# Six of batch 0's last groups are moved from ahead of the tile loop into tiles 0 to 3, and batch 1's first input loads are issued between filter copies

## The chip, the cores and the metric

One Trainium2 chip, one core. The metric is the device time of one execution in microseconds (us), lower is better. Names of engines in the profile: PE is TensorE's matmuls and PEld its weight loads, DVE is VectorE, ACT is ScalarE, POOL is GpSimd and SP is SyncE, which issues most of the DMAs.

## The reference

A global filter over the sequence in the frequency domain, then a two-layer network with exact GELU over every token:

```
x: (8, 3008, 256); filt_r, filt_i: (1505, 256); w_in: (256, 2048); w_out: (2048, 256); all float32
X = rfft(x, axis=1)
Y = X * (filt_r + 1j * filt_i)
y = irfft(Y, n=3008, axis=1)
h = y.reshape(24064, 256) @ w_in
g = 0.5 * h * (1 + erf(h / sqrt(2)))
out = g @ w_out            # (24064, 256) float32
```

## The kernel before

**The filter as matmuls.** 3008 = 47 × 64, so a transform of one batch goes in four matrix stages. For batch 0 they are called c1, c2, c3 and c4, and stand ahead of the network with nothing of the network beside them; the order of the instructions is written out by hand. c1 turns input columns by a table, c1t transposes on PE, c2 multiplies by the second table, and DVE's product with the filter (L569) follows it. c3 turns back and leaves its result in the tile vt. Then come eight groups u = 0 to 7. For each, c3t(u) makes eight 128 × 128 transposes on PE, which DVE copies to a tile d (L605). c4(u) makes two halves of four matmuls of 94 columns on d, and each half is written to a ring of mixed tokens (376 columns a group, channels on the partitions) by ACT or DVE (L620). The filter tile F is loaded by POOL's DMAs to half of the partitions, and dup_filters copies it to the other half, two planes a copy, mostly on POOL.

**Later batches.** Batches 1 to 7 use s1, s2, s3 and s4, in slots amid the network. fold adds and subtracts input halves on DVE; s1 (four steps a batch) multiplies by the table T1s and stores to R1 in DRAM; r1 loads it back as b; s2 (three steps u) multiplies by T2p; s2_out takes the product with the filter's rearranged copy Fu on DVE (L467); s2_sum adds; s3 multiplies by U and stores to R2; r2 loads it as d; s4 multiplies by T4a and writes the ring. Fu is made of F by move_filters: 16 DMAs on SP's queue ahead of the tiles, and 20 more in slot 18. The tables T1s, T2p (table_2_parities), pick and U (table_u) for the later batches are made on POOL, most of them in slot 9.

**The network.** 47 tiles t of 512 tokens. mm1(t, jc), for 16 steps jc, multiplies two halves (dc) of the ring's channels by w_in into a PSUM bank, and ACT takes the GELU into g (L643). The second layer for the tile before goes beside it: mm2_first (64 matmuls of 256 columns) for tiles 0 to 2, mm2_seven from tile 3 on, a form with seven products for eight, which needs sums of w_out's quarters (weight_sums, four operations on DVE, result w_sums, in slot 20) and sums of g (sums_1, sums_2, sums_3 on DVE).

**What sets the order.** A slot is s = 16·t + jc. Each slot first runs what was put there, then its share of the second layer, then its mm1:

```
    for s in range((NT + 1) * 16):
        t, jc = s // 16, s % 16
        for f, a in at.pop(s, ()):
            f(*a)
```

For batch 1 the slots are s1 at 4, 8, 11, 13; r1 at 17; s2 at 27, 41, 54; s3 11 or 12 slots after its s2. Each engine runs its own instructions in this order, and waits where a semaphore holds it. SP issues DMAs in order too, each on the next of eight completion lanes, and waits for the lane's DMA before. POOL does the same with its DMAs; those move input, weights, and most outputs. PSUM after the head has three banks "h" (mm1), two "o" (second layer) and three "f".

Of the kernel before, what the change touches and what calls it, by code (L numbers as in the profile page):

```python
# [19 lines left out]
K1 = 24  # L20
HB = 32
# [10 lines left out]
class _Mix:  # L32
    def __init__(self, ctx, tc, x, filt_r, filt_i, w_in, w_out, out):
        self.tc, self.nc = tc, tc.nc
        self.x, self.filt_r, self.filt_i = x, filt_r, filt_i
        self.w_in, self.w_out, self.out = w_in, w_out, out
        self.B, self.S, self.D = x.shape
        self.DFF = w_in.shape[1]
        assert self.S == NA * NB and self.D == 256 and self.DFF == 2048
        pool = lambda name, bufs, **kw: ctx.enter_context(tc.tile_pool(name=name, bufs=bufs, **kw))  # L40
        P = bass.MemoryType.PSUM
        self.const = pool("const", 1)
        self.px = pool("px", 1)
# [12 lines left out]
        self.T1 = c.tile([2 * NA, 96], BF16, name="T1")
        self.T2p = c.tile([128, K1, 2, 2, 16], BF16, name="T2p")
        self.xs = c.tile([128, 4, 256], BF16, name="xs")
        self.U = c.tile([128, 2, 2 * HB], BF16, name="U")
        self.T4c = c.tile([96, NA, 2], BF16, name="T4c")  # L60
        self.F = c.tile([128, 2, K1, 256], BF16, name="F")
        self.Fu = c.tile([128, 2, 2, 6, 256], BF16, name="Fu")
        f = self.F.rearrange("p t k c -> p (t k c)")
        self.s4_sb = f[:, 0:2048].bitcast(FP16).rearrange("p (i n) -> p i n", i=8)
        self.v_sb = [f[:, o:o + 1024].rearrange("p (c d) -> p c d", c=2) for o in (2048, 3072)]
        self.T4a = f[0:96, 4096:7168].rearrange("p (w m) -> p w m", w=HB)
        self.w_in_sb = c.tile([128, 2, self.DFF], BF16, name="w_in_sb")
        self.w_out_sb = c.tile([128, 16, self.D], FP16, name="w_out_sb")
        self.w_sums = c.tile([128, 4, 8, 128], FP16, name="w_sums")
        self.ps, self.st = {}, {}  # L70
        self.flip = 0
# [22 lines left out]
    def load_x_pairs(self, b, c, h, n=1):  # L94
# [3 lines left out]
        for v in range(2):  # L98
# [478 lines left out]
    def c3(self, p, np=2):  # L577
# [11 lines left out]
        for half in range(2):  # L589
            v = self.vt[:, half, 0:96, :].rearrange("c a b -> c (a b)").rearrange("c (n k) -> c n k", n=HB)  # L590
            self._evac(v[:, :, 8 * p:8 * p + 8 * np], ps[half][:, 0:256 * np].rearrange("c (k n) -> c n k", n=HB),
                       False if p == 11 and half else "act")

    def c3t(self, u):

        if u % 2 == 0:
            self.st[0, "d", u // 2] = self.pd.tile([96, 8, 256], BF16, tag="d", name="d_sb")
        d = self.st[0, "d", u // 2]
        ps = self.bank("ps_c3t", "f", BF16)
        for i in (0, 2, 4, 6, 1, 3, 5, 7):  # L600
            o = 96 * (4 * u + i // 2)
            self.nc.tensor.transpose(ps[:, 128 * i:128 * i + 128],
                                     self.vt[:, i % 2].rearrange("c a b -> c (a b)")[:, o:o + 128], self.eye)
        n = 4 * (u % 2)
        self._evac(d[:, n:n + 4, :].rearrange("p a b -> p (a b)"), ps[0:96], False)  # L605

    def c4(self, u, eng):

        if u == 0:

            self.ring = self.py.tile([128, 2, 2 * self.S], BF16, tag="y", name="y_sb")
        d = self.st[0, "d", u // 2]
        for half in range(2):
            ps = self.bank("ps_c4", "h" if (2 * u + half) % 5 < 3 else "o")
            for i in range(4):
                self.nc.tensor.matmul(ps[:, 94 * i:94 * i + 94],
                                      lhsT=d[:, 4 * (u % 2) + i, 128 * half:128 * half + 128],
                                      rhs=self.T4c.rearrange("p a b -> p (a b)"), start=True, stop=True)
            yv = self.ring[:, half, GRP * u:GRP * u + GRP].rearrange("c (m w) -> c m w", w=4)
            self._evac(yv, ps[:, 0:376].rearrange("c (i m) -> c m i", i=4), eng[half], 1.0 / self.S)  # L620
# [10 lines left out]
    def mm1(self, t, jc):  # L631
        nc = self.nc
        if jc == 0:
            self.st["g", t] = self.pg.tile([128, 16, TCH], FP16, tag="g", name="g_sb")
        ps = self.bank("ps_h", "h")
        w = self.w_in_sb[:, :, 256 * (jc // 2) + jc % 2:256 * (jc // 2) + 256:2]
        o = 0
        for off, n in self.segs(t):
            for dc in range(2):
                nc.tensor.matmul(ps[:, o:o + n], lhsT=w[:, dc],  # L640
                                 rhs=self.ring[:, dc, off:off + n], start=(dc == 0), stop=(dc == 1))
            o += n
        nc.scalar.activation(out=self.st["g", t][:, jc, :], in_=ps, func=AF.Gelu)  # L643
# [139 lines left out]
def kernel(  # L783
# [31 lines left out]
    m.ones = g.tile([128, 512], BF16, name="ones")  # L815
# [12 lines left out]
    m.vt = m.pg.tile([128, 2, 97, 32], BF16, tag="g", name="vt_sb")  # L828
    for k, n in ((0, 6), (6, 8), (14, 10)):
        m.load_filters(k, n)  # L830
    m.load_w_in()

    nc.gpsimd.memset(m.vt[:, :, 96, :], 0.0)
# [21 lines left out]
    m.table_3(1)  # L855
    m.dup_filters(nc.vector, 0, 2)
# [4 lines left out]
    m.dup_filters(nc.gpsimd, 6, 18)  # L861
# [30 lines left out]
    m.table_1_tiles(g)  # L892
    for c in (0, 2):
        for h in range(2):
            m.load_x_pairs(1, c, h, 2)
    m.load_w_out(0)
    m.load_w_out(8)

# [4 lines left out]
    for u in range(10):  # L903
        if u < 8:
            m.c3t(u)
        if u >= 2:
            m.c4(u - 2, (False if u > 7 else act, act))
# [11 lines left out]
    for b in range(1, B):  # L919
        hi = first(b)  # L920
        e = 4 * (b == B - 1)
        s1, n1, r1 = (4, 3.3, 17) if b == 1 else (hi - 87, 3.7, hi - 73) if b == 2 else (hi - 94 - e, 3.7, hi - 80 - e)
        s2 = (27, 41, 54) if b == 1 else (hi - 74, hi - 59, hi - 44) if e else (hi - 64 + (b == 2), hi - 48, hi - 32)
        busy.update(range(s1 - 1, s1 + int(3 * n1) + 2))
        for c in range(4):
            slot = (4, 8, 11, 13)[c] if b == 1 else s1 + int(c * n1)
            put((0, 1, 5, 8)[c] if b == 1 else (70, 74, 86, 94)[c] if b == 2 else hi - 94 - (20, 13, 8, 6)[c], m.fold, b, c)
            put(slot, m.s1, b, c)
        for u in range(3):
            put(r1 if u < 2 else s2[0] + 1, m.r1, b, u)  # L930
            put(s2[u], m.s2, b, u)
            for i in range(4):
                put(s2[u] + 2 * i + (b == 2 and u == 0), m.s2_out, b, u, i // 2, i % 2)
            for i in range(2):
                put(s2[u] + (9 + i if 1 < b < B - 1 else 7 + 2 * i), m.s2_sum, b, 2 * u + i)
            s3 = s2[u] + ((11, 11, 12)[u] if b == 1 else 12 if e or (b, u) in ((2, 0), (B - 2, 2)) else 13)
# [46 lines left out]
    put(18, m.move_filters, 2, 4)  # L983
    put(20, m.weight_sums)
# [56 lines left out]
```

## Time and profile before

| | |
|---|---|
| time, three runs | 734.16, 734.37 (median), 734.50 us |
| span of the profiled execution | 732.0 us; its own time is not among the runs' records, and the median lies 2.4 us above the span |
| PE busy | 713.6 us (97%), 9016 matmuls |
| DVE busy | 597.0 us (82%) |
| ACT busy | 576.5 us (79%) |
| POOL busy | 286.2 us (39%) |
| granted TensorE clock | 0.999 |
| DMA, mean over the span | 120 GB/s |

The span runs from the first to the last instruction. The share of busy time is a mean over stages: for the first 38 us there is no network, and its stages are limited by DVE, ACT and the loads in turn; afterwards PE runs matmuls nearly without a gap. A line of a timeline gives the start, the time to the end of the last of the merged instructions, the engine, the source line, the operation, output and input tiles with shapes, and the count; in brackets stands the idle time before it and what ended that.

### The profile page before, as it was taken

What the parts mean: (1) busy time and instruction counts of PE and PEld (TensorE: products, weight loads), DVE (VectorE), ACT (ScalarE), POOL (GpSimd) and SP (SyncE); (2) the same over time, 40 slices, a digit from 0 to 9 for tenths busy, and PEclk for the clock granted to TensorE, in tenths of its full rate; (3) what the DMA queues carried; (4) which work ended last, traced back from release to release, by engine and by line L of the source; (5) the groups of instructions that cost most, each with busy time, mean ns of one, the idle gap of its engine ahead of it and who ended that gap; (6) DMA issues with size and microseconds to landing.
All of it is one profiled execution on the core that took longest, in us unless ns stands there. A gap on an engine that the chain in (4) does not pass through costs nothing.

```text
span 732.0 us, 22073 instructions
## 1 busy us (share of the span) xinstructions
PE 713.6 (97%) x9016; PEld 505.9 (69%) x9165; DVE 597.0 (82%) x1091; ACT 576.5 (79%) x1050; POOL 286.2 (39%) x546
## 2 busy tenths in 40 slices
PE   7999999999999999999999999999999999999997
PEld 4846675676777666666677667666677767777776
DVE  8975698899878998798976999779988897775666
ACT  7997778688877888778887788877888788877773
POOL 7853377864223452135511364115531121121121
PEclk9999999999999999999999999999999999999999
DMA  9886544765355553646535455355545442411011
GB/s 158 160 173 161 155 89 123 201 124 100 88 169 143 120 112 107 178 99 134 128 107 162 114 132 119 97 149 151 110 102 135 141 117 84 114 47 42 30 59 59
DMA packets 81254, 87.72 MB, mean 120 GB/s; under 512 B 13393, under 2 KB 61137, under 8 KB 81153
## 3 DMA queue, kind: packets, MB, share of 16 engines
q0 software_dynamic: 22288, 39.50, 24.3%
q1 hardware_dynamic: 58449, 46.62, 23.8%
q8 instruction: 71, 1.16, 0.7%
q14 instruction: 30, 0.25, 0.1%
q10 hardware_dynamic: 416, 0.20, 0.1%
HBM read 54.00 MB, written 46.66 MB: 138 GB/s over the span
## 4 chain that ended last, share of the span: by engine, by line
PE 86%; DVE 4%; DMA 4%; issue 2%; POOL 2%; ACT 1%; DVEq 0%; POOLq 0%; ACTq 0%
PE ps_o L714 38%; PE ps_h L640 38%; PE ps_s L514 3%; PE ps_o L656 2%; PE ps_s L429 2%; PE ps_s L487 2%; DMA x_sb<-in_x_dram 2%; PE ps_s L456 2%; DVE s_sb L685 1%; DMA w_out_sb<-in_moe_w_out_dram 1%; POOL F L137 1%; DMA F<-in_filt_i_dram 1%; ACT g_sb L643 1%; DVE p L467 1%; POOL x_sb L92 1%
## 5 line engine op out<-in xcount | busy, mean ns | idle before, releaser
L643 ACT ACTIVATE g_sb<-ps_h 128x512 f16<-128x512 f32 x752 | 446.4, 601 | 139.9 <-PE ps_h L640 115.5
L640 PE MATMUL ps_h<-y_sb,w_in_sb 128*128 128x512 bf16 (+3 forms) x1455 | 415.0, 365 | 1.5 <-DVE p L467 0.7
L761 POOL DMA_DIRECT2D out_dram<-ost x231 | 131.4, 575 | 388.0 <-DVE ost L743 361.3
L714 PEld LDWEIGHTS <-g_sb 128*128 128x128 f16 x2816 | 184.4, 98 | 80.7 <-issue 14.6
L640 PEld LDWEIGHTS <-w_in_sb 128*128 128x128 bf16 x1600 | 126.3, 98 | 8.3 <-issue 2.4
L714 PE MATMUL ps_o<-w_sums,g_sb 128*128 128x128 f16 x1408 | 121.7, 219 | 1.7 <-DVE g_sb L691 0.2
L714 PE MATMUL ps_o<-w_sums,s_sb 128*128 128x128 f16 x1408 | 121.2, 219 | 1.6
L714 PEld LDWEIGHTS <-s_sb 128*128 128x128 f16 x1408 | 95.1, 98 | 37.6 <-issue 2.5
L685 DVE TENSOR_TENSOR s_sb<-g_sb 128x1024 f16<-128x1024 f16 x176 | 116.4, 692 | 0.4 <-ACT g_sb L643 0.3
L714 PE MATMUL ps_o<-w_out_sb,g_sb 128*128 128x128 f16 x1408 | 113.7, 219 | 1.8
L467 DVE TENSOR_TENSOR p<-ps_s,Fu 128x1024 bf16<-128x1024 f32 x84 | 101.5, 1216 | 9.1 <-PE ps_s L456 6.5
L101 POOL DMA_DIRECT2D x_sb<-in_x_dram x156 | 79.4, 515 | 3.1 <-issue 1.6
L691 DVE TENSOR_TENSOR g_sb<-s_sb,g_sb 128x1024 f16<-128x1024 f16 x88 | 60.3, 687 | 1.5
L714 PE MATMUL ps_o<-w_out_sb,F 128*128 128x128 f16 x704 | 60.6, 219 | 0.9
L696 DVE TENSOR_TENSOR F<-g_sb 128x1024 f16<-128x1024 f16 x88 | 61.4, 697 | 0.0
L714 PEld LDWEIGHTS <-F 128*128 128x128 f16 x704 | 47.1, 98 | 14.6 <-issue 0.4
L736 DVE TENSOR_TENSOR t_sb<-t_sb,ps_o 128x256 f32<-128x256 f32 x44 | 18.4, 417 | 39.0 <-PE ps_o L714 38.6
L514 PEld LDWEIGHTS <-d_sb 96*128 96x128 bf16 x448 | 31.4, 97 | 26.8 <-issue 1.3
L325 ACT ACTIVATE F<-ps_s 128x512 bf16<-128x512 f32 x83 | 45.5, 607 | 0.1
L325 ACT ACTIVATE y_sb<-ps_s 128x376 bf16<-128x376 f32 x95 | 45.4, 478 | 0.1
L327 DVE CAST a_sb<-ps_s 128x512 bf16<-128x512 f32 x54 | 34.7, 684 | 12.0 <-PE ps_s L429 11.7
L743 DVE TENSOR_TENSOR ost<-t_sb,ps_o 128x256 f32<-128x256 f32 x86 | 32.1, 414 | 13.7 <-PE ps_o L714 13.7
(160 smaller groups left out, 589.2 us busy)
## 6 DMA issues: line engine op xcount, KB each, us to landing
out_dram<-ost POOLq DMA_DIRECT2D x127, 128.0 KB, 2.9
b_sb<-R SPq DMA_DIRECT2D x21, 512.0 KB, 5.1
R<-F SPq DMA_DIRECT2D x84, 128.0 KB, 2.5
d_sb<-R SPq DMA_DIRECT2D x56, 192.0 KB, 4.3
R<-a_sb SPq DMA_DIRECT2D x108, 96.0 KB, 2.2
x_sb<-in_x_dram POOLq DMA_DIRECT2D x48, 94.0 KB, 2.7
x_sb<-in_x_dram POOLq DMA_DIRECT2D x48, 48.0 KB, 2.8
x_sb<-in_x_dram POOLq DMA_DIRECT2D x12, 188.0 KB, 5.0
```

The lines of the kernel that those rows point to most:

```text
L101: self.nc.gpsimd.dma_start(out=xt[64 * v + to:64 * v + to + m, h, 4 * c:4 * c + 4 * n, :], in_=xv[h][at:at + m, w:w + 4 * n, :])
L325: self.nc.scalar.activation(out=out, in_=in_, func=AF.Copy, scale=1.0 if scale is None else scale)
L327: self.nc.vector.tensor_copy(out=out, in_=in_)
L467: v(out=w[:, a], in0=ps.unsqueeze(2).to_broadcast([128, 2, 2, 256]), in1=f.unsqueeze(1).to_broadcast([128, 2, 2, 256]), op=ALU.mult)
L514: nc.tensor.matmul(ps[:, 94 * i:94 * i + 94], lhsT=d[:, (grp % 2) * 4 + i, 128 * half:128 * half + 128], rhs=self.T4a[:, 4 * grp + i, 0:2 ...
L640: nc.tensor.matmul(ps[:, o:o + n], lhsT=w[:, dc], rhs=self.ring[:, dc, off:off + n], start=(dc == 0), stop=(dc == 1))
L643: nc.scalar.activation(out=self.st["g", t][:, jc, :], in_=ps, func=AF.Gelu)
L685: self.nc.vector.tensor_tensor(out=self.st["s", t][:, i:i + 2], in0=a, in1=b, op=ALU.subtract)
L691: self.nc.vector.tensor_tensor(out=a21[:, k], in0=self.st["s", t][:, k, 0], in1=a22[:, k], op=ALU.add)
L696: self.nc.vector.tensor_tensor(out=self.s4_sb[:, k], in0=a12[:, k], in1=s2[:, k], op=ALU.subtract)
L714: nc.tensor.matmul(ps[:, (m + 1) % 2, sub, :], lhsT=a[:, i, 128 * sub:128 * sub + 128], rhs=b[:, i], start=i == 0, stop=i == 7)
L761: eng.dma_start(out=out, in_=tile_[lo - r0:lo - r0 + n])
```

## The change

c3t and c4 for groups 0 and 1 stay ahead of the tiles; group 2's c3t goes to slot 6. Groups 3, 4 and 5, and 6 and 7, get three DMA transposes on SP's queue (c3t_dma, from vt straight to d) in slots 2, 10 and 45. Their c4 halves go to twelve slots from 11 to 63, all evicted by DVE. c4 takes one half a call. The first three mm1 are split: their first halves (dc = 0) run ahead of slot 0. vt is laid out in blocks of 128 with its own memory that outlives the head, with zeros set by two larger memsets on POOL among the filter loads; T2p and w_sums now lie in that memory, so table_2_parities goes to slot 15 and weight_sums to slot 54. Batch 1's input loads: two stand ahead of POOL's filter copies, two after the fifth of them, the rest after the copies; w_out's loads follow, and T1s comes after those. For batch 1, s1 goes to slots 3, 8, 13, 18; r1 to 20; s2 to 32, 44, 56; s3 to nine slots after its s2; s2_out and s2_sum to other steps after s2; the other tables to slots 15 and 24, move_filters to slot 21.

```diff
@@ -54,7 +54,6 @@
...
         self.T1 = c.tile([2 * NA, 96], BF16, name="T1")
-        self.T2p = c.tile([128, K1, 2, 2, 16], BF16, name="T2p")
         self.xs = c.tile([128, 4, 256], BF16, name="xs")
...
@@ -66,7 +65,11 @@
...
         self.w_out_sb = c.tile([128, 16, self.D], FP16, name="w_out_sb")
-        self.w_sums = c.tile([128, 4, 8, 128], FP16, name="w_sums")
+        vt = c.tile([128, HB * 256], BF16, name="vt_sb")
+        self.vt = vt.rearrange("p (w h k) -> p w h k", w=HB, h=2)
+        self.T2p = vt[:, 0:64 * K1].rearrange("p (k r q j) -> p k r q j", r=2, q=2, j=16)
+        self.w_sums = vt[:, 3072:7168].bitcast(FP16).rearrange("p (q i n) -> p q i n", q=4, i=8)
+        self.ahead, self.begun = {}, set()
         self.ps, self.st = {}, {}
...
@@ -91,11 +94,11 @@
...
-    def load_x_pairs(self, b, c, h, n=1):
+    def load_x_pairs(self, b, c, h, n=1, vs=(0, 1)):
...
         xv = self.x[b].rearrange("(n1 h w) d -> h n1 w d", h=2, w=HB)
-        for v in range(2):
+        for v in vs:
             for to, at, m in ((0, 23, 24), (24, 0, 23)) if h else ((0, 0, NA),):
...
@@ -587,37 +590,42 @@
...
         for half in range(2):
-            v = self.vt[:, half, 0:96, :].rearrange("c a b -> c (a b)").rearrange("c (n k) -> c n k", n=HB)
-            self._evac(v[:, :, 8 * p:8 * p + 8 * np], ps[half][:, 0:256 * np].rearrange("c (k n) -> c n k", n=HB),
+            self._evac(self.vt[:, :, half, 8 * p:8 * p + 8 * np], ps[half][:, 0:256 * np].rearrange("c (k n) -> c n k", n=HB),
                        False if p == 11 and half else "act")
+    def d_tile(self, i):
+        if (0, "d", i) not in self.st:
+            self.st[0, "d", i] = self.pd.tile([128, 8, 256], BF16, tag="d", name="d0_sb")
+        return self.st[0, "d", i]
+
     def c3t(self, u):
-        if u % 2 == 0:
-            self.st[0, "d", u // 2] = self.pd.tile([96, 8, 256], BF16, tag="d", name="d_sb")
-        d = self.st[0, "d", u // 2]
+        d = self.d_tile(u // 2)
         ps = self.bank("ps_c3t", "f", BF16)
         for i in (0, 2, 4, 6, 1, 3, 5, 7):
-            o = 96 * (4 * u + i // 2)
-            self.nc.tensor.transpose(ps[:, 128 * i:128 * i + 128],
-                                     self.vt[:, i % 2].rearrange("c a b -> c (a b)")[:, o:o + 128], self.eye)
+            self.nc.tensor.transpose(ps[:, 128 * i:128 * i + 128], self.vt[:, 4 * u + i // 2, i % 2], self.eye)
         n = 4 * (u % 2)
-        self._evac(d[:, n:n + 4, :].rearrange("p a b -> p (a b)"), ps[0:96], False)
-
-    def c4(self, u, eng):
-
-        if u == 0:
+        self._evac(d[0:96, n:n + 4, :].rearrange("p a b -> p (a b)"), ps[0:96], False)
+
+    def c3t_dma(self, u, n):
+
+        d, k = self.d_tile(u // 2), 4 * (u % 2)
+        self.nc.sync.dma_start_transpose(out=d[:, k:k + 4 * n].rearrange("p w (h c) -> p (w h) c", h=2),
+                                         in_=self.vt[:, 4 * u:4 * u + 4 * n].rearrange("c w h k -> c (w h k)"))
+
+    def c4(self, u, half, eng, tag="f"):
+
+        if u == half == 0:
...
         d = self.st[0, "d", u // 2]
-        for half in range(2):
-            ps = self.bank("ps_c4", "h" if (2 * u + half) % 5 < 3 else "o")
-            for i in range(4):
-                self.nc.tensor.matmul(ps[:, 94 * i:94 * i + 94],
-                                      lhsT=d[:, 4 * (u % 2) + i, 128 * half:128 * half + 128],
-                                      rhs=self.T4c.rearrange("p a b -> p (a b)"), start=True, stop=True)
-            yv = self.ring[:, half, GRP * u:GRP * u + GRP].rearrange("c (m w) -> c m w", w=4)
-            self._evac(yv, ps[:, 0:376].rearrange("c (i m) -> c m i", i=4), eng[half], 1.0 / self.S)
+        ps = self.bank("ps_c4", tag)
+        for i in range(4):
+            self.nc.tensor.matmul(ps[:, 94 * i:94 * i + 94],
+                                  lhsT=d[0:96, 4 * (u % 2) + i, 128 * half:128 * half + 128],
+                                  rhs=self.T4c.rearrange("p a b -> p (a b)"), start=True, stop=True)
+        yv = self.ring[:, half, GRP * u:GRP * u + GRP].rearrange("c (m w) -> c m w", w=4)
+        self._evac(yv, ps[:, 0:376].rearrange("c (i m) -> c m i", i=4), eng, 1.0 / self.S)
...
@@ -628,18 +636,22 @@
...
-    def mm1(self, t, jc):
+    def mm1(self, t, jc, part=0):
         nc = self.nc
-        if jc == 0:
+        if ("g", t) not in self.st:
             self.st["g", t] = self.pg.tile([128, 16, TCH], FP16, tag="g", name="g_sb")
-        ps = self.bank("ps_h", "h")
         w = self.w_in_sb[:, :, 256 * (jc // 2) + jc % 2:256 * (jc // 2) + 256:2]
         o = 0
+        ps = self.ahead.pop(jc, None) or self.bank("ps_h", "h")
         for off, n in self.segs(t):
-            for dc in range(2):
+            for dc in range(1 if jc in self.begun and t == 0 else 0, part or 2):
                 nc.tensor.matmul(ps[:, o:o + n], lhsT=w[:, dc],
...
             o += n
+        if part:
+            self.ahead[jc] = ps
+            self.begun.add(jc)
+            return
         nc.scalar.activation(out=self.st["g", t][:, jc, :], in_=ps, func=AF.Gelu)
...
@@ -812,7 +824,7 @@
...
     m.load_x(16, 16)
-    m.ones = g.tile([128, 512], BF16, name="ones")
+    m.ones = m.pg.tile([128, 512], BF16, tag="g", name="ones")
     nc.vector.memset(m.ones, 1.0)
...
@@ -825,12 +837,13 @@
...
     m.T3, m.T3i = t3[:, 0], t3[:, 1]
-    m.vt = m.pg.tile([128, 2, 97, 32], BF16, tag="g", name="vt_sb")
     for k, n in ((0, 6), (6, 8), (14, 10)):
         m.load_filters(k, n)
+        if k < 14:
+            w = 16 * (k // 6)
+            nc.gpsimd.memset(m.vt[:, w:w + 16, :, 96:128].bitcast(FP32), 0.0)
     m.load_w_in()
-    nc.gpsimd.memset(m.vt[:, :, 96, :], 0.0)
...
@@ -853,12 +866,15 @@
...
     m.table_3(1)
+    m.load_x_pairs(1, 0, 0, 2)
     m.dup_filters(nc.vector, 0, 2)
...
     m.dup_filters(nc.vector, 2, 2)
-    m.dup_filters(nc.gpsimd, 6, 18)
+    m.dup_filters(nc.gpsimd, 6, 10)
+    m.load_x_pairs(1, 0, 1, 2, (0,))
+    m.dup_filters(nc.gpsimd, 16, 8)
     m.move_filters(0, 2)
...
@@ -889,22 +905,25 @@
...
     m.table_u_rows(g)
-    m.table_1_tiles(g)
-    for c in (0, 2):
-        for h in range(2):
-            m.load_x_pairs(1, c, h, 2)
+    m.load_x_pairs(1, 0, 1, 2, (1,))
+    for h in range(2):
+        m.load_x_pairs(1, 2, h, 2)
     m.load_w_out(0)
     m.load_w_out(8)
+    m.table_1_tiles(g)
...
     m.psum(ctx, h=(3, 1), o=(2, 1), f=(3, 1))
-    for u in range(10):
-        if u < 8:
-            m.c3t(u)
-        if u >= 2:
-            m.c4(u - 2, (False if u > 7 else act, act))
+    m.c3t(0)
+    m.c3t(1)
+    m.c4(0, 0, act, "o")
+    m.c4(0, 1, False, "o")
+    m.c4(1, 0, act)
+    m.c4(1, 1, False)
+    for jc in range(3):
+        m.mm1(0, jc, 1)
...
@@ -919,21 +938,21 @@
...
         e = 4 * (b == B - 1)
-        s1, n1, r1 = (4, 3.3, 17) if b == 1 else (hi - 87, 3.7, hi - 73) if b == 2 else (hi - 94 - e, 3.7, hi - 80 - e)
-        s2 = (27, 41, 54) if b == 1 else (hi - 74, hi - 59, hi - 44) if e else (hi - 64 + (b == 2), hi - 48, hi - 32)
+        s1, n1, r1 = (3, 5, 20) if b == 1 else (hi - 87, 3.7, hi - 73) if b == 2 else (hi - 94 - e, 3.7, hi - 80 - e)
+        s2 = (32, 44, 56) if b == 1 else (hi - 74, hi - 59, hi - 44) if e else (hi - 64 + (b == 2), hi - 48, hi - 32)
         busy.update(range(s1 - 1, s1 + int(3 * n1) + 2))
         for c in range(4):
-            slot = (4, 8, 11, 13)[c] if b == 1 else s1 + int(c * n1)
-            put((0, 1, 5, 8)[c] if b == 1 else (70, 74, 86, 94)[c] if b == 2 else hi - 94 - (20, 13, 8, 6)[c], m.fold, b, c)
+            slot = (3, 8, 13, 18)[c] if b == 1 else s1 + int(c * n1)
+            put((0, 4, 9, 14)[c] if b == 1 else (70, 74, 86, 94)[c] if b == 2 else hi - 94 - (20, 13, 8, 6)[c], m.fold, b, c)
             put(slot, m.s1, b, c)
...
             for i in range(4):
-                put(s2[u] + 2 * i + (b == 2 and u == 0), m.s2_out, b, u, i // 2, i % 2)
+                put(s2[u] + (i + i // 2 if b == 1 else 2 * i + (b == 2 and u == 0)), m.s2_out, b, u, i // 2, i % 2)
             for i in range(2):
-                put(s2[u] + (9 + i if 1 < b < B - 1 else 7 + 2 * i), m.s2_sum, b, 2 * u + i)
-            s3 = s2[u] + ((11, 11, 12)[u] if b == 1 else 12 if e or (b, u) in ((2, 0), (B - 2, 2)) else 13)
+                put(s2[u] + (5 + i if b == 1 else 9 + i if b < B - 1 else 7 + 2 * i), m.s2_sum, b, 2 * u + i)
+            s3 = s2[u] + (9 if b == 1 else 12 if e or (b, u) in ((2, 0), (B - 2, 2)) else 13)
             put(s3, m.s3, b, u)
...
@@ -967,12 +986,18 @@
...
-    put(9, lambda: m.gate(m.st["x1"][0:1, 1, 15, 0:1]))
-    put(9, m.table_2_parities)
-    put(9, m.table_u_pick, g)
-    put(9, m.table_4_rows, g)
-    put(9, m.weights_4, g)
-    put(23, m.table_u)
+    put(2, m.c3t_dma, 3, 1)
+    put(6, m.c3t, 2)
+    put(10, m.c3t_dma, 4, 2)
+    put(45, m.c3t_dma, 6, 2)
+    for i, s in enumerate((11, 12, 21, 22, 25, 26, 38, 39, 50, 51, 62, 63)):
+        put(s, m.c4, 2 + i // 2, i % 2, False)
+    put(15, lambda: m.gate(m.st["x1"][0:1, 1, 15, 0:1]))
+    put(15, m.table_2_parities)
+    put(15, m.table_u_pick, g)
+    put(15, m.table_4_rows, g)
+    put(15, m.weights_4, g)
+    put(24, m.table_u)
     put(49, m.table_4_factors, g)
...
@@ -980,8 +1005,8 @@
...
         put(slot, m.table_4_all, parts[2 * i:2 * i + 2])
-    put(18, m.move_filters, 2, 4)
-    put(20, m.weight_sums)
+    put(21, m.move_filters, 2, 4)
+    put(54, m.weight_sums)
     plain = (0, 1, 2)
...
```

## The prediction

> **What bounds the kernel now.** Slot means 16 × tile + step of the loop that orders tiles; c3t and c4 are batch 0's last transposes and last matmuls, of which eight groups (0 to 7) stand ahead of tile 0. Times are microseconds from the span's start.
>
> First the page: PE is busy 97% of 732.0, so only PE's idle time at the head, work added to PE, and new waits of PE can move the time. Next the timeline from 26 to 42, where PE's idle time lies:
>
> ```profile
> 31.34 5.56 DVE L327 COPY d_sb<-ps_c3t 96x1024 bf16<-96x1024 bf16 x8 [0.75 <-PE ps_c3t L602]
> 32.46 5.53 ACT L325 ACTIVATE y_sb<-ps_c 128x376 bf16<-128x376 f32 x14 [0.50 <-PE ps_c L616]
> 36.82 1.06 DVE L329 TENSOR_SCALAR y_sb<-ps_c 128x376 bf16<-128x376 f32 x2
> 37.30 1.94 PE L640 MATMUL ps_h<-y_sb,w_in_sb 128*128 128x512 bf16 x7
> 37.99 2.06 ACT L643 ACTIVATE g_sb<-ps_h 128x512 f16<-128x512 f32 x4
> ```
>
> For six microseconds the eight groups go at the pace of their evictions (0.69 each on DVE, 0.40 on ACT); the first GELU comes at 37.99. Then PE's own timeline:
>
> ```profile
> 44.02 0.60 PE L656 MATMUL ps_o<-w_out_sb,g_sb 128*128 128x256 f16 x4 [0.32 <-DMA w_out_sb<-in_moe_w_out_dram]
> 47.37 0.63 PE L429 MATMUL ps_s<-x_sb,T1s 47*64 47x512 bf16 x8
> ...
> 78.75 0.27 PE L391 MATMUL ps_t<-eye,T1g 47*96 47x47 bf16 x2
> ...
> 81.73 0.64 PE L487 MATMUL ps_s<-p,U 32*64 32x256 bf16 x32
> ```
>
> From 44.02 (slot 10) PE hardly idles again. The rows fix slots: 47.37 is slot 13, 78.75 slot 49, 81.73 slot 52; a full slot is 0.87. Third, SP's timeline, past which the transposes are queued:
>
> ```profile
> 53.57 0.82 SPq L444 DMA_DIRECT2D b_sb<-R  x2
> 54.44 14.73 SPq L130 DMA_DIRECT2D Fu<-F  x20
> 69.27 2.75 SPq L761 DMA_DIRECT2D out_dram<-ost  x3
> 72.13 0.33 SPq L444 DMA_DIRECT2D b_sb<-R  x1
> 72.97 1.77 SPq L761 DMA_DIRECT2D out_dram<-ost  x2
> 74.87 2.46 SPq L497 DMA_DIRECT2D R<-F  x4
> ```
>
> SP issues without a pause from 53.57 to 77.33. Last, the chain of waits from 80 to 115:
>
> ```profile
> 87.03 3.47 DVE p L467 x3
> 90.50 0.49 DVE s_sb L685
> ...
> 96.57 2.02 DVE F L696
> 98.60 1.40 DVE xs L109
> ...
> 109.47 0.69 DVE g_sb L691
> 110.22 0.79 PE ps_o L714 x11
> ```
>
> DVE's timeline has no idle entry from 86.42 to 110.5, and PE waits for DVE at 110.22 (0.20). So DVE has no slack there, though PE is the bound on both sides.
>
> **The change part by part.** *The head.* Only groups 0 and 1 stay. POOL now issues two loads of batch 1 amid its filter copies (1.0) and two longer memsets; the product that needs the delayed copy has about 0.5 in hand, so I put 0.5 on the head (bounds 0 and 1.0). Then two d evictions from 31.84 end at 33.23, c4 of group 1 reaches ACT at 33.6 and is out at 34.1; three half mm1 of 0.22 and the other half of the first, plus the 0.26 that GELU followed mm1 by, put the first GELU at 35.2, 2.8 earlier. In before, PE was ready for slot 10 5.71 after the first GELU and then waited 0.32 for w_out. With the same two s1 ahead of slot 10 and half of three mm1 done, I take 5.5: slot 10 at 40.7, gain 3.3. That needs w_out by then. In before it landed 8.02 after its issue at 35.96, some 4 of that behind batch 1's input. With 4 of those 12 loads gone early, input should be through near 36 and w_out land near 40; bounds 39 and 44. The group 2 transposes (0.43, slot 6) hide beside ACT, whose GELUs set those slots.
>
> *PE's added work.* Twelve halves of c4 go into slots where PE is the bound. The nearest row is s4, four matmuls of 94 columns: 107.44 to 107.60, 0.165 each. 12 × 0.165 = 2.0, 1.3 of it before slot 50. T1s, the T2 and U tables move later behind fold; table_u would be ready within 0.1 of PE's arrival, priced at 0 (to 0.5).
>
> *SP and the transposes.* s1 of step 3 goes from slot 13 to 18: 40.7 + 6 slots × 0.87 + 2 × 0.72 (there mm2 is thinner) + one s1 0.55 + two c4 0.34 = 48.25. R1's stores then no longer queue behind those of step 2, so the b loads follow 5.65 after instead of 6.2, at 53.9, 0.3 later than before. SP's unchanged string of 30 DMAs stands ahead of the transpose of groups 6 and 7, which is thus issued at 77.33 + 0.3 = 77.65. PE reaches slot 50, whose c4 reads it, at 79.9 − 3.3 + 1.3 = 77.9. [...] By the nearest row, a lone 512 KB load on this queue, it takes 4.1 or 4.6 to land:
>
> ```profile
> b_sb<-R SPq DMA_DIRECT2D x1, 512.0 KB, 4.1
> ```
>
> The lower end is the fastest Fu move, 1.9; the upper one is Fu's slope (32 KB 3.2, 64 KB 4.4, so 16 times 32 KB some 21). I take 4.4, as size and queue are that row's: landing at 82.05, PE waits 4.1. Behind that wait stand all of PE's later matmuls, and GELU behind them. The transposes of group 3 (issued near 32, read at slot 21, near 51) and of 4 and 5 (issued near 42.6, read near 54) have over 11 and cost nothing at 4.4; at 21 the latter cost too.
>
> [...]
>
> *DVE.* w_sums now lies in vt's memory, so its four sums leave the idle stretch at 49.03 (to 51.95, 2.9) for slot 54, behind the copy of s3 at slot 53 and ahead of s2's products at slot 56. From the landing: slot 53 at 82.05 + 2 × 0.165 + 3 × 0.87 = 85.0; copy done 1.5 later (81.73 to 83.2 in before) at 86.5; sums to 89.4; one output copy 0.61; four products × 1.16 to 94.65, against 90.42: 4.2 late. Group 7's two evictions (0.53 each) add 1.1, so DVE is 5.3 late at 110.22, where it had no slack. PE alone would be −3.3 + 2.0 + 4.1 = 2.8 late; it waits another 2.5 for DVE.
>
> Sum: **+5.3**. It is made on the profiled span, 732.0; the runs' median is 734.37, and the 2.4 around the span I leave as they are: 739.7.
>
> **The rivals.** *One: the landing costs nothing* (transpose issued 4 earlier, or landing within 0.3). Then slot 53 comes at 80.9 and the DVE reckoning gives +1.2: 735.6. Against it: SP's string has no gap to shrink.
>
> *Two, not slower: DVE's stretch has give as well.* In before its F and fold rows from 96.57 to 104 took 2.02, 1.47, 1.19, 1.47 where the same forms take 0.68 elsewhere, beside POOL's table products: 3.4 lost. If the new order keeps these apart and the transpose is in time, only PE's account stays: −3.3 + 2.0 = −1.3, 733.1; with 4.1 at the head (no filter delay, w_out by 39.5) −2.1, 732.3. It decides when w_sums ends by 84 and PE never waits at slot 50. Against it: the gate that starts POOL's products follows DVE's own sums, so both shift together.
>
> *Three: the head gives nothing.* Group 3's transpose and Fu moves take DMA time from w_out, and slot 10 stays at 44.0: +3.3 on the forecast, 743.0. For it: the DMA share is 0.94 to 1.21 from 32 to 44. [...]
>
> *Four: transposes at the upper end.* At 21, groups 4 and 5 land at 63.6, 9.3 after slot 25 wants them; R1's last store waits for the same lane, so b loads go at 66.2 and slot 32 waits 2 more; groups 6 and 7 land at 111, 21.8 after slot 50. With 2.5 for DVE: +34, 768.
>
> **How the numbers follow.** Forecast 0.46, one 0.14, two 0.24, three 0.12, four 0.04. About 0.2% (1.5) is what a measurement can tell from no change. Two lies on both sides of −1.5: 0.16 faster, 0.08 same; one: 0.09 same, 0.05 slower. So faster 0.16, same 0.17, slower 0.67. The range runs from 732.2, two's upper gain, to 744.0, which is three, or a landing of 8.7; outside lie four and the tails, together 0.15. The forecast's own range is 737 to 743 (landing 1.9 to 7.7).
>
> **What would show it.** First GELU near 35.2 and slot 10 near 40.7 (head); PE idle for some 4 at c4 of group 6, released by the transpose (SP); that transpose issued at 77 to 78, right behind four R stores; w_sums behind a copy of s3, and s2's last products ending 4 later than 90.4; PE waiting on DVE over tiles 4 and 5. No PE idle at slot 50 makes the forecast wrong by its largest term; PE ahead of before at slot 82 makes it wrong in sign.

## The result, and the profile after

Six runs of the changed kernel took 747.69 to 755.26 us, median 754.37; six of before, beside them, 734.31. The ratio is 1.0261, with a 95% interval of 1.0241 to 1.0281: slower by 20 us, where the forecast was slower by 5.3 (739.7, at most 744.0). The sign held, the size did not. The profiled execution is one of the longer ones, 755.23; its span, 753.5, is 21.5 above that of before, and the account below is of these 21.5.

The page of after, its span and the row of granted clocks in 40 slices:

```profile
span 753.5 us, 22144 instructions
...
PEclk9989889999999999999999999999999999999999
```

The digits 8 in the third, fifth and sixth slice (18.8 us each) are new; in before the mean clock was 0.999, here it is 0.988. So PE's clock was lowered somewhere between 38 and 57, and again between 75 and 113.

The timeline of all engines from 30 to 43 answers the one shown of before for the head:

```profile
32.27 1.28 DVE L330 COPY d_sb<-ps_c3t 96x1024 bf16<-96x1024 bf16 x2 [0.75 <-PE ps_c3t L606]
32.42 2.08 SPq L613 DMA_TRANSPOSE d_sb<-vt_sb  x1
...
33.02 1.57 POOL L163 DMA_DIRECT2D w_out_sb<-in_moe_w_out_dram  x2
...
35.64 1.58 ACT L655 ACTIVATE g_sb<-ps_h 128x512 f16<-128x512 f32 x3 [1.17 <-PE ps_h L648]
```

The first GELU comes at 35.64, 2.35 earlier than in before, and w_out's loads are issued at 33.02, 2.9 earlier. The head is shorter, by 0.45 less than the 2.8 that was forecast: its first d eviction starts at 32.27 (31.34 in before), 0.93 later, where 0.5 had been put for batch 1's loads amid POOL's filter copies. PE's own timeline shows what became of it:

```profile
40.42 1.04 PE L648 MATMUL ps_h<-y_sb,w_in_sb 128*128 128x512 bf16 x4
49.28 1.01 PE L668 MATMUL ps_o<-w_out_sb,g_sb 128*128 128x256 f16 x4 [7.82 <-DMA w_out_sb<-in_moe_w_out_dram]
50.08 1.06 PE L648 MATMUL ps_h<-y_sb,w_in_sb 128*128 128x512 bf16 x2
...
87.63 0.59 PE L648 MATMUL ps_h<-y_sb,w_in_sb 128*128 128x512 bf16 x2
96.49 0.49 PE L624 MATMUL ps_c<-T4c,d_sb 96*128 96x94 bf16 x4 [8.27 <-DMA d_sb<-vt_sb]
96.78 1.06 PE L668 MATMUL ps_o<-w_out_sb,g_sb 128*128 128x256 f16 x4
97.63 1.06 PE L648 MATMUL ps_h<-y_sb,w_in_sb 128*128 128x512 bf16 x2
```

The reader should see two idle times of 8, at slot 10 for w_out and at slot 50 for the transpose of groups 6 and 7, and that behind each of them the same pair of matmuls (L648, x2) takes 1.06 where it took 0.59 (at 87.63). Stretches of the clock show the second effect (columns: stretch, length, busy time of PE, PEld, DVE, ACT and POOL, granted clock, DMA share, GB/s):

```profile
44.00:48.00 4.00, 0.00 (x0) 0.00 (x0) 1.39 (x2) 0.00 (x0) 0.00 (x0) 0.70 1.10 221
48.00:52.00 4.00, 2.72 (x14) 1.74 (x14) 0.51 (x1) 0.60 (x1) 0.00 (x0) 0.50 0.91 107
52.00:56.00 4.00, 4.00 (x34) 2.24 (x33) 2.27 (x5) 2.65 (x5) 0.00 (x0) 0.94 0.60 120
...
88.00:92.00 4.00, 0.22 (x2) 0.00 (x0) 1.33 (x4) 0.80 (x3) 1.84 (x4) 0.75 0.94 256
...
100.00:104.00 4.00, 4.00 (x56) 2.51 (x55) 1.80 (x3) 3.14 (x7) 0.00 (x0) 0.97 0.00 0
```

The clock fell to half during the idle time (0.70 over 44 to 48 is full speed until 45.6 and half from there) and stayed there until 52.5, as the 0.94 says, 3.2 after PE had resumed. Those 3.2 did half their work, so 1.6 were lost. Around slot 50 it was half from 90.0 (0.75 over 88 to 92) to 100.2 (0.97 over 100 to 104), 3.75 of it after PE had resumed: 1.9 lost.

SP's timeline:

```profile
38.13 11.59 SPq L441 DMA_DIRECT2D R<-a_sb  x8
50.23 3.58 SPq L613 DMA_TRANSPOSE d_sb<-vt_sb  x1
...
65.19 0.83 SPq L447 DMA_DIRECT2D b_sb<-R  x2
66.06 14.83 SPq L133 DMA_DIRECT2D Fu<-F  x20
81.00 4.30 SPq L773 DMA_DIRECT2D out_dram<-ost  x5
85.41 0.53 SPq L447 DMA_DIRECT2D b_sb<-R  x1
86.04 2.45 SPq L500 DMA_DIRECT2D R<-F  x4
88.53 5.87 SPq L613 DMA_TRANSPOSE d_sb<-vt_sb  x1
```

and the chain of waits from 80 on:

```profile
87.94 0.55 SPq L500
88.48 0.05 issue
88.53 7.91 DMA d_sb<-vt_sb
96.45 0.05 issue
96.49 0.49 PE ps_c L624 x4
```

The transpose stands behind the R stores as the prediction had it, and takes 7.91 to land.

**Where the 21 went.** The start of the same GELU in both traces (counted from 0, so that GELU 12 lies behind slot 11) gives the lag, after's start minus before's, at any place:

| GELU | before | after | lag | what lies between, in after |
|---|---|---|---|---|
| 9 | 44.22 | 41.86 | -2.36 | the head |
| 12 | 47.48 | 53.95 | +6.47 | wait for w_out 7.82 (0.32 in before), half clock 1.6, two halves of c4, one s1 (0.55) moved on |
| 48 | 78.91 | 87.07 | +8.16 | that s1, six halves of c4 |
| 51 | 81.84 | 100.58 | +18.74 | wait for the transpose 8.27, half clock 1.9, two halves of c4 |
| 81 | 112.35 | 133.24 | +20.89 | two halves of c4, waits for DVE |
| 751 | 721.84 | 742.75 | +20.91 | nothing |

-2.36 + 7.5 + 1.6 + 8.27 + 1.9 + 12 × 0.165 + 1.8 is 20.7, which leaves 0.2 of the 20.9 open. The 1.8 is what the last growth of 2.15 leaves beside its two halves of c4; it is put down to DVE, for which PE waits 0.96 at 129.29. The end behind the last GELU adds 0.6 to the span (732.0 to 753.5).

### The profile page after: what moved, and what is told of

Same layout as the page of the kernel before. It is cut to its first block, busy times and chain, and to the rows that moved or that the text cites. A ratio compares the mean times of both kernels' runs of the same rounds, so it can differ in the third digit from the quotient of the medians.

```text
span 753.5 us, 22144 instructions
## 1 busy us (share of the span) xinstructions
PE 724.9 (96%) x9125; PEld 505.4 (67%) x9125; DVE 600.8 (80%) x1098; ACT 572.0 (76%) x1038; POOL 286.9 (38%) x547
## 3 DMA queue, kind: packets, MB, share of 16 engines
q8 instruction: 71, 1.16, 0.7%
## 4 chain that ended last, share of the span: by engine, by line
PE 84%; DMA 7%; DVE 3%; POOL 3%; SPq 1%; issue 1%; ACT 0%; DVEq 0%; POOLq 0%
PE ps_h L648 39%; PE ps_o L726 35%; PE ps_s L517 2%; DMA w_out_sb<-in_moe_w_out_dram 2%; PE ps_s L432 2%; PE ps_s L490 2%; PE ps_o L668 1%; PE ps_s L459 1%; DMA x_sb<-in_x_dram 1%; DVE p L470 1%; SPq L133 1%; DMA d_sb<-vt_sb 1%; POOL x_sb L104 1%; POOL F L140 1%; DMA b_sb<-R 1%
## 5 line engine op out<-in xcount | busy, mean ns | idle before, releaser
L648 PE MATMUL ps_h<-y_sb,w_in_sb 128*128 128x512 bf16 (+3 forms) x1600 | 447.4, 367 | 1.1 <-DVE p L470 0.7
L648 PEld LDWEIGHTS <-w_in_sb 128*128 128x128 bf16 x1600 | 126.7, 98 | 8.4 <-issue 2.1
L726 PE MATMUL ps_o<-vt_sb,g_sb 128*128 128x128 f16 x1408 | 121.7, 219 | 0.5 <-DVE g_sb L703 0.2
L726 PE MATMUL ps_o<-vt_sb,s_sb 128*128 128x128 f16 x1408 | 121.2, 219 | 0.0
L726 PEld LDWEIGHTS <-s_sb 128*128 128x128 f16 x1408 | 95.1, 98 | 37.7 <-issue 2.5
```

The lines of the kernel that those rows point to most:

```text
L648: nc.tensor.matmul(ps[:, o:o + n], lhsT=w[:, dc], rhs=self.ring[:, dc, off:off + n], start=(dc == 0), stop=(dc == 1))
L726: nc.tensor.matmul(ps[:, (m + 1) % 2, sub, :], lhsT=a[:, i, 128 * sub:128 * sub + 128], rhs=b[:, i], start=i == 0, stop=i == 7)
```

## Experiments

The theory to be tested: (1) group 3's transpose, in flight beside w_out's load, holds the load back; (2) the transpose of groups 6 and 7 is late because of what is queued ahead of it on SP; (3) each wait of 8 costs nearly 2 more, because the clock is at half behind it; (4) w_sums' four sums in slot 54 make DVE another 2 to 3 late.

### Group 3 by PE, or by DMA at slot 10

pe3:

```diff
-    put(2, m.c3t_dma, 3, 1)
+    put(8, m.c3t, 3)
```

> Group 3 is transposed by PE (c3t, slot 8) and no longer by DMA at slot 2; all else as in after. Theory (the transpose of group 3 shares the DMA engines packet by packet with w_out's load and holds it back): w_out lands near 41.5, PE's wait of 7.8 at slot 10 goes and with it the stretch of half clock behind it (1.6), PE pays 0.43 for eight transposes: 754.4 - 9.0 = 745.4, and the wait of 8.3 for groups 6 and 7 at slot 50 stays. Rival (w_out is late because the R stores of s1 now come forward to 38, or because batch 1's remaining x loads stand ahead of it): slot 10 stays at 47 to 49, 752 to 755.

late3:

```diff
-    put(2, m.c3t_dma, 3, 1)
...
+    put(10, m.c3t_dma, 3, 1)
     put(10, m.c3t_dma, 4, 2)
```

> Group 3's DMA transpose is kept, but issued at slot 10 just ahead of that of groups 4 and 5. Theory: as with PE's transpose, slot 10 near 41.5 and 745.0, since w_out has landed when the transpose starts; c4 of group 3 at slot 21 still finds it landed. Rival (the R stores of s1 take the place of the transpose beside w_out): slot 10 at 44 to 46 and 748 to 751. If the transpose at this place delays the R stores and the loads of b behind it, s2 at slot 32 waits and PE shows an idle time there.

Measured: pe3 747.83 (ratio to before 1.0187, 1.0172 to 1.0203), late3 747.26 (1.0179, 1.0163 to 1.0194). Both are 2.3 to 2.4 above what was expected, but both rivals fall in their main claim: PE no longer waits for w_out to speak of. PE's timeline of late3 at slot 10:

```profile
41.51 0.60 PE L668 MATMUL ps_o<-w_out_sb,g_sb 128*128 128x256 f16 x4 [0.28 <-DMA w_out_sb<-in_moe_w_out_dram]
```

At GELU 12 the lag is -2.83 (pe3 -2.23) where after has +6.47: changes of 9.3 and 8.7, where 9.0 was expected. In late3 the R stores were issued at 37.9, beside w_out's load, and did not make PE wait. What late3 gave back was lost at slot 50, where it waits longer and the clock stays at half longer. PE's waits in late3 (us in total, times, longest):

```profile
PE ps_c L624 <- DMA d_sb<-vt_sb: 8.8, 1, 8.8
```

That is 0.55 more than in after. The clock was at half from 83.55 to 93.78, 6.04 of it after PE had resumed at 87.74, so 3.0 were lost where after lost 1.9; 0.9 of that lies behind GELU 51. It makes up the whole difference in the next stretch, where the lag grows by 3.04 (GELU 51 to 81) and by 2.15 in after.

### What a transpose does to a load, by itself

before_t8:

```diff
+        self.scr = c.tile([128, 8, 128], BF16, name="scr_sb")
...
+    put(2, lambda: nc.sync.dma_start_transpose(
+        out=m.scr, in_=m.vt[:, 0].rearrange("c a b -> c (a b)")[:, 0:1024]))
```

> The kernel before, with one DMA transpose of 128 x 1024 bf16 (256 KB, as group 3's) from vt into an unused tile added on SP at slot 2; nothing reads the copy. Theory (a transpose in flight beside w_out's load holds the load back): w_out lands 4 to 8 later than 43.98, PE idles at slot 10 for as long, with 1 to 2 of half clock behind it: 739 to 744. Rival (w_out is late in after for another reason, the transpose costs what its 256 KB cost): 734.4 to 735.5.

before_c8:

```diff
+        self.scr = c.tile([128, 8, 128], BF16, name="scr_sb")
...
+    put(2, lambda: nc.sync.dma_start(
+        out=m.scr, in_=m.vt.rearrange("c h a b -> c (h a b)")[:, 0:2048].rearrange(
+            "c (i n) -> c i n", i=8)[:, :, 0:128]))
```

> The kernel before, with the same 256 KB moved at the same place in the same 1024 pieces of 256 bytes by an ordinary DMA from vt into the unused tile. Theory (it is the transpose, not the bytes or the size of the pieces): 734.4 to 735.5, w_out at most 1 later. Rival (any 1024 small pieces beside w_out hold it back): as with the transpose, 739 to 744.

Measured: before_t8 742.13 (1.0114, 1.0099 to 1.0129), before_c8 735.59 (1.0024, 1.0014 to 1.0033), before 733.75 beside them. The DMA issues between 26 and 60 (last column: median us from issue to landing) of before, before_t8 and before_c8:

```profile
w_out_sb<-in_moe_w_out_dram POOLq DMA_DIRECT2D x2, 512.0 KB, 9.4
```

```profile
w_out_sb<-in_moe_w_out_dram POOLq DMA_DIRECT2D x2, 512.0 KB, 14.5
...
scr_sb<-vt_sb SPq DMA_TRANSPOSE x1, 15.2
```

```profile
w_out_sb<-in_moe_w_out_dram POOLq DMA_DIRECT2D x2, 512.0 KB, 10.8
...
scr_sb<-vt_sb SPq DMA_DIRECT2D x1, 256.0 KB, 14.5
```

One transpose that nobody reads makes before 8.4 slower. PE waits 4.90 for w_out at slot 10 (0.32 in before, 0.58 in before_c8):

```profile
48.59 0.37 PE L657 MATMUL ps_o<-w_out_sb,g_sb 128*128 128x256 f16 x1 [4.90 <-DMA w_out_sb<-in_moe_w_out_dram]
```

GELU 12 lags by 7.37, some 2.7 of it by the clock, which is at half until 53.92. The plain copy of the same bytes in the same 1024 pieces takes nearly as long to land, 14.5, but PE starts slot 10 at 44.67, 0.65 later than in before; the run is 1.8 longer. So it is the transpose, not its bytes.

How it does so is visible in part, in the packets (the pieces in which the DMA engines move a transfer). In after from 42 to 45 the trace has 377 packets of w_out and 363 of 256 bytes of the transpose; in before_c8 from 41 to 44, 490 of w_out and 321 of the copy; in before in the same stretch 595 of w_out. Beside a transpose w_out thus ran at 126 packets per us, beside a copy at 163, alone at 198. Why w_out then goes at some 30 to 60 packets per us once the transpose's packets are through (46 to 51 in after, where the DMA share is 0.33 and 0.30 from 48 to 50) stays open.

How much is lost also changes from run to run: PE's wait for w_out was 7.8 in after's profile, 6.6 in early67's and 3.0 in mid67's (both below, like fill), with the same transpose in slot 2, and after's own runs spread over 7.6. The traces show what goes with it: which of the two is issued first, SP's transpose or the first half of w_out on POOL's queue. In after, early67 and before_t8 the transpose is ahead, by 0.6, 1.2 and 3.9, and that half lands 16.2, 15.1 and 13.1 after its issue. In mid67 and fill it is 0.4 and 0.6 behind, and the half lands after 11.5 and 11.4 (8.7 in late3, where no transpose is near). The slow end of w_out's load shows in the first three alone. No run set this order by design, so it is a pattern of five profiles and not a test.

### The transpose of groups 6 and 7 earlier in SP's queue

early67:

```diff
     put(10, m.c3t_dma, 4, 2)
-    put(45, m.c3t_dma, 6, 2)
+    put(10, m.c3t_dma, 6, 2)
```

> The transpose of groups 6 and 7 is issued at slot 10 right behind that of groups 4 and 5 and no longer at slot 45 behind the Fu moves, a 512 KB load of b and four stores of R; group 3's stays at slot 2. Theory (it lands late only because of what is queued ahead of it on SP, 512 KB and four times 128 KB): the wait of 8.3 at slot 50 and the half clock behind it (1.9) go: 754.4 - 10.2 = 744.2, less up to 0.5 for DVE. Rival (DVE's clump of weight sums sets the place): PE waits on DVE at tile 5 for 3 to 4 more than now and the time is 747 to 748. A second rival (longer transposes in the SP queue delay the R stores of s1 and the b loads): PE idles at slot 32 for 2 to 4, 746 to 748.

mid67:

```diff
-    put(45, m.c3t_dma, 6, 2)
...
     put(21, m.move_filters, 2, 4)
+    put(22, m.c3t_dma, 6, 2)
```

> After, with the transpose of groups 6 and 7 issued at slot 22: still behind the 20 Fu moves on SP, but ahead of the five stores of the output, the 512 KB load of b and the four 128 KB stores of R. Theory (of the 8 that it took to land, some 4 went by behind the b load and the R stores on SP's queue, and 16 tiles alone need some 4): issued near 81, landed by 86, PE finds it at slot 50 (88.2): no wait there and 744 as with early67. Rival (sixteen tiles need 8 at this point, whatever is ahead of them): landed at 89, PE waits 1 and the stretch of half clock does not come: 745 to 746.

Measured: early67 744.24 (1.0131, 1.0078 to 1.0183), mid67 743.62 (1.0136, 1.0117 to 1.0155); 744.2 and 744 were expected. In both PE does not wait for the transpose any more. early67's median is met by luck, though: its four runs took 739.22, 741.28, 747.20 and 747.34, and the profiled one is that of 747.20. In it the lag grows by 0.53 from GELU 48 to 51, where after's grows by 10.58: 10.05 saved there, as forecast (10.2). But 0.95 more than in after is lost from GELU 12 to 48 and 1.29 more from 51 to 81, which is what the two rivals said, in small. mid67's DMA issues from 76 to 84 tell the landing of 16 tiles when nothing large is ahead of it on the queue, and of what follows it:

```profile
b_sb<-R SPq DMA_DIRECT2D x1, 512.0 KB, 7.3
...
R<-F SPq DMA_DIRECT2D x1, 128.0 KB, 7.0
...
d_sb<-vt_sb SPq DMA_TRANSPOSE x1, 3.9
```

3.9, where it was 7.91 in after behind that b load and four R stores. The packets agree: in after the first of the transpose's 2048 starts 3.8 after the issue and half of them only from 94.9 on, when those of the b load (until 92.5) and of the R stores (until 94.1) are through; in mid67 the first starts after 1.2 and the last ends 2.05 later. POOL's input loads, which were in flight beside it in after (until 95.1), may have a share; no run separates them. In the eight profiles where 16 tiles went at slots 10 to 22 and the landing is known they landed in 3.8 to 5.9. The rival (16 tiles need 8 wherever they stand) falls. But mid67 shows what is late next. In its timelines DVE's copy of s3 waits for the landing of R's stores, and PE for what hangs on that:

```profile
91.90 0.69 DVE L330 CAST F<-ps_s 128x512 bf16<-128x512 f32 x1 [6.64 <-DMA R<-F]
```

```profile
91.97 0.59 PE L648 MATMUL ps_h<-y_sb,w_in_sb 128*128 128x512 bf16 x2 [2.76 <-ACT F L328]
```

Its lag grows by 6.1 from GELU 51 (3.69) to GELU 66 (9.77), where after's grows by 1.3. That mid67 met the expected 744 is luck too, two misses that cancel: w_out cost 4.8 less in it and this stretch 4.8 more. The verdict on the landing rests on the rows, not on the time.

### Both at once, and w_sums

late3_early67:

```diff
-    put(2, m.c3t_dma, 3, 1)
...
+    put(10, m.c3t_dma, 3, 1)
     put(10, m.c3t_dma, 4, 2)
-    put(45, m.c3t_dma, 6, 2)
+    put(10, m.c3t_dma, 6, 2)
```

> Both: groups 3, 4 and 5, 6 and 7 transposed by DMA in a row at slot 10. Theory: both waits and both stretches of half clock go, 754.4 - 9.0 - 10.2 = 735.2, that is about as fast as before (734.3): 2.4 gained at the head against 2.0 for twelve halves of c4 and some 1.5 on DVE. Rivals: the R stores take the transpose's place beside w_out (738 to 741); the transposes in a row delay the b loads and s2 at slot 32 (737 to 739).

both_sums27 is that kernel with

```diff
-    put(54, m.weight_sums)
+    put(27, m.weight_sums)
```

> As late3_early67 (all DMA transposes at slot 10, 739.6), with w_sums' four sums moved from slot 54 to slot 27, where DVE idles. Theory (at slot 54 they stand behind a copy that waits and ahead of s2's products, and make DVE 3 late): the lag between slots 51 and 81 (1.05 to 6.01 behind before) falls by 2.5 to 3.2: 736.5 to 737. Rival (the late Fu moves and stores of R set that stretch): 739 to 739.6.

Measured: late3_early67 739.60 (1.0070, 1.0053 to 1.0087), clock 1.00: both waits are gone and 14.8 of the 20 with them. It is 4.4 above what was expected. PE's waits have these two entries:

```profile
PE ps_h L648 <- DVE p L470: 2.2, 2, 1.6
...
PE ps_s L459 <- DMA b_sb<-R: 0.9, 1, 0.9
```

The second is the second rival: three transposes in a row keep SP for 5.66, and the b loads are issued at 57.02 (53.57 in before). The first is mostly w_sums: its longer part, 1.6 at 92.31, is gone when they are moved, and 0.7 is left, as in before. both_sums27 took 736.84 (1.0040, 1.0025 to 1.0055), 2.8 less, as expected. The intervals of the two ratios just overlap, but the rows are clear: from GELU 51 to 81 the lag grows by 2.19, where late3_early67's grows by 4.96. The other 1.6 of the 4.4 has no test of its own; the 0.9 for b is part of it. DVE's timeline of after shows where the sums stood:

```profile
102.16 0.69 DVE L330 CAST F<-ps_s 128x512 bf16<-128x512 f32 x1 [2.57 <-PE ps_s L490]
102.77 0.68 DVE L683 TENSOR_TENSOR vt_sb<-w_out_sb 128x1024 f16<-128x1024 f16 x1
...
105.90 4.61 DVE L470 TENSOR_TENSOR p<-ps_s,Fu 128x1024 bf16<-128x1024 f32 x4
```

Behind a copy that DVE idled for, ahead of the four products that s3 waits for.

### The clock

fill:

```diff
+    def fill(self, n):
+        ps = self.bank("ps_fill", "f")
+        for i in range(n):
+            self.nc.tensor.matmul(ps, lhsT=self.w_in_sb[:, 0, 0:128], rhs=self.w_in_sb[:, 0, 0:512],
+                                  start=True, stop=True)
...
+    put(10, m.fill, 32)
+    put(50, m.fill, 33)
```

> After, with dummy matmuls of 128x512 in the two waits: 32 ahead of slot 10's products and 33 ahead of slot 50's c4, some 6.9 and 7.1 at 0.216 each, which end before the transfers land at 49.3 and 96.5. Both transfers come as late as before, but PE is not idle. Theory (each idle wait of 8 costs 1.6 to 1.9 more, because the granted clock falls to 0.5 and stays there for 3.2 to 3.8 after PE has resumed): clock 1.00, 754.4 - 3.5 = 750.9. Rival (the slow stretch is caught up again, or DVE sets the end): 753.5 to 754.5.

Measured: 751.61, 2.8 less than after, and a clock of 0.999. The stretches of fill beside those shown of after:

```profile
44.00:48.00 4.00, 4.00 (x20) 1.85 (x19) 0.00 (x0) 0.00 (x0) 0.00 (x0) 1.00 1.21 206
48.00:52.00 4.00, 4.00 (x38) 2.31 (x37) 1.21 (x3) 1.70 (x4) 0.00 (x0) 1.00 0.97 244
```

PE did 65 matmuls of no use and the median fell by 2.8. The total alone does not show the clock's price: the intervals of the two ratios overlap (1.0226 to 1.0260 in fill, 1.0241 to 1.0281 in after), w_out's first half had landed at 44.6 in fill's profile, 3.8 before the dummies ended, and the transpose took 9.3 from its issue at 85.34. PE's timeline of fill:

```profile
48.35 0.60 PE L675 MATMUL ps_o<-w_out_sb,g_sb 128*128 128x256 f16 x4
...
94.68 0.34 PE L631 MATMUL ps_c<-T4c,d_sb 96*128 96x94 bf16 x4 [1.61 <-DMA d_sb<-vt_sb]
```

The rows behind the waits do show it: from slot 10's first product to GELU 12 it is 4.67 in after (49.28 to 53.95) and 3.14 in fill (48.35 to 51.49), from slot 50's c4 to GELU 51 4.09 (96.49 to 100.58) and 2.29 (94.68 to 96.97). The same matmuls are 1.5 and 1.8 shorter at full clock, beside 1.6 and 1.9 worked out above.

### Can putting groups off pay?

six_tuned puts off six groups, with the slots of before for batch 1:

```diff
...
+    put(10, m.c3t_dma, 3, 1)
...
+    put(14, m.c3t_dma, 4, 2)
+    put(14, m.c3t, 6)
+    put(16, m.c3t, 7)
...
-    put(54, m.weight_sums)
+    put(20, m.weight_sums)
...
```

> Six groups put off as in after, but group 3 transposed by DMA at slot 10, 4 and 5 by DMA at slot 14 behind the stores of s1's last step, 6 and 7 by PE at slots 14 and 16; s1, r1, s2, s3, the copies around them and w_sums (slot 20) at the slots of before. Theory (what both_sums27 still lost, 3, is the transposes' 6 in the SP queue ahead of R and b, which made the Fu moves late): head -2.8, twelve halves of c4 +2.0, sixteen transposes on PE +0.9, two evictions hidden: 0.1 from before, 734 to 735. Rival (w_out now lands at 42 and s1 at the old slots makes SP late again): 736 to 737.

two_tuned puts off two:

```diff
...
+    for u in range(8):
+        if u < 6:
+            m.c3t(u)
...
+    put(14, m.c3t_dma, 6, 2)
+    for i, s in enumerate((50, 51, 62, 63)):
+        put(s, m.c4, 6 + i // 2, i % 2, False)
...
```

> Only groups 6 and 7 are put off: c3t and c4 of groups 0 to 5 stand ahead of tile 0, one DMA transpose of groups 6 and 7 at slot 14, their four halves of c4 in slots 50, 51, 62, 63; loads of batch 1 amid the filter copies as in after; all other slots as in before, w_sums at 23. Theory: the head gains two evictions of 0.69, the four halves cost 0.7, nothing waits: -0.7, 733.1 to 734. Rival (the transpose of 16 tiles ahead of the b loads makes s2 late, or w_out sets slot 10 whatever the head does): 734.5 to 736.

Measured: six_tuned 737.72 (1.0057, 1.0039 to 1.0074), two_tuned 734.15 beside 734.12 (0.9999, 0.9991 to 1.0008). Neither beats before. six_tuned missed both expectations: w_out came in time, but the halves of c4 waited for ACT's copies of s1 and s3, with which they share nothing but the PSUM banks "f". That is 1.8 of the 3.6 by which it lags at the last GELU; the rest is not taken apart. Its PE timeline:

```profile
44.42 0.33 PE L624 MATMUL ps_c<-T4c,d_sb 96*128 96x94 bf16 x4 [0.62 <-ACT a_sb L328]
...
70.44 0.33 PE L624 MATMUL ps_c<-T4c,d_sb 96*128 96x94 bf16 x4 [1.16 <-ACT F L328]
```

two_tuned missed both too, if by little: the 0.7 that it was to gain is not there. PE has no wait in it that before lacks, and the account is bare: the lag is -0.67 at GELU 12, -0.34 behind the first two halves of c4 and 0.01 behind the other two. The head gained 0.67 (0.32 of it PE's wait for w_out, which is gone) and the four halves cost 0.66, as forecast; 0.5 is added by GELU 81. So it is the head that fell short of the 1.4 forecast for two evictions:

```profile
32.50 3.99 DVE L330 COPY d_sb<-ps_c3t 96x1024 bf16<-96x1024 bf16 x6 [0.75 <-PE ps_c3t L606]
```

Six evictions take 3.99 where before's eight took 5.56, but the first starts 1.16 later than in before (31.34). All ten kernels with batch 1's loads among POOL's filter copies start it late, at 31.77 to 32.50; before, before_t8 and before_c8 start it at 31.33 to 31.73. In two_tuned the copies end at 29.05, in before at 27.16. By these rows, putting the loads there costs much of what putting groups off gains; no run moved the loads alone, so this stays argued.

## Why the prediction was wrong in size

*The head and PE's added work* held but for 0.9 of the gain of 3.3. The first GELU was forecast at 35.2 and came at 35.64, which is the first eviction's 32.27 for 31.84; PE was ready for slot 10 at 41.46, not 40.7. The twelve halves were put at 0.165 each, and in two_tuned a pair costs 0.33 to 0.35.

*"w_out land near 40; bounds 39 and 44"* is the first step that failed: 49.28. The range came from before's own load with less in front of it, and nothing in it stood for the transpose issued 0.6 ahead of the load. The prediction asked of that transpose only whether it would be in time for its own reader ("cost nothing at 4.4"), not what it does to others. Rival three named it among the causes and priced it at 44.0, where w_out had been; with 49.28 and the clock it was 7 more. pe3, late3 and before_t8 show that it is the transpose.

*"I take 4.4, as size and queue are that row's: landing at 82.05, PE waits 4.1"* is the second. SP's order held, and the transpose's issue came 0.3 after PE's arrival where 0.25 before was forecast. For the transfer alone 4.4 was good: mid67 has 3.9. But before has no DMA transpose: the row it was taken from is a load with nothing ahead of it, and here a 512 KB load and four stores of 128 KB had been issued on the same queue within some 3 us. The landing took 7.91, and PE waited 8.27. Rivals one and two, which had no wait here, fall with it, and so does four with its landing of 21.

*The clock* was in no term of the sum. The two waits of 8 drew 3.5 with them, and fill's rows show 3.3 of it.

*DVE*: 2.5 of waiting beyond PE's own lateness was forecast; the lag grows by 2.15 from GELU 51 to GELU 81, 0.33 of it c4, so 1.8. That w_sums behind s3's copy and ahead of the products make DVE late is shown in late3_early67, by moving them. What they cost in after itself no run measured: PE's wait of 0.96 at 129.29, about half of the 1.8, stays in both_sums27 (0.94), so it is hardly theirs.

Term by term: w_out 7.5 and its clock 1.6 more than forecast, and 0.9 less gained at the head than 3.3; the transpose 4.2 and its clock 1.9 more; DVE 0.7 less; behind the last GELU 0.6. That is 16.0 of the 16.2 between +5.3 and the spans' +21.5.

By the traces, 16 tiles landed in 3.9 in mid67 and eight in 3.2 in late3, so in these runs the time does not go by the tile; the 3.9 agrees with the 4.1 of the 512 KB load whose row the forecast took. What a transpose does to a load beside it is another matter: PE waits 4.90 for w_out in before_t8 and 0.58 in before_c8.

## What to carry to other kernels

A DMA that is put beside a load on the critical path is priced by what it does to that load, not only by when it is needed itself: one transpose that nobody reads made before 8.4 slower. Its landing time went with the queue it joined, 7.91 right behind a 512 KB load and four stores of 128 KB (after) and 3.9 ahead of them (mid67), so count the bytes issued just ahead of it. A stall of PE that may last several us costs more than its length, by half of the time for which the granted clock stays down behind it: 1.6 to 3.0 in the stalls of 2.8 to 8.8 here. Work that is hidden ahead of a PE-bound loop costs its full PE time once it is inside: the four halves put off in two_tuned cost 0.66, and its head gained 0.67.

## What the runs showed of the hardware

- 16 tiles of 128 × 128 by DMA transpose landed in 3.9 in mid67, with 32 KB and 64 KB moves just ahead of them on the queue, and 8 tiles in 3.2 in late3. 8 tiles beside the loads of x and w_out took 13.0 to 17.0. SP itself was held 1.4 to 5.9 by one issue.
- With a transpose of 256 KB beside a 1 MB load, PE waited 2.7 to 7.5 longer for that load (mid67, after); with a plain copy of the same pieces, 0.3 longer (before_c8).
- From the first GELU on, the granted clock fell to 0.5 in each of PE's eight waits of 2.76 to 8.82 (after, pe3, late3, early67, mid67, before_t8), or within 0.6 behind it, and in none of those up to 1.61 (fill). In after it fell 4.2 and 1.8 after PE fell idle, and came back 3.2 and 3.75 after PE had resumed; the two stretches lasted 6.83 and 10.24, two and three times 3.41, and mid67's two lasted 3.41 each.
